# One two-bank PSUM tile, or two one-bank tiles, for the value product of a memory-attention and SwiGLU kernel

## The chip, the cores and the metric

The kernel runs on one core of one Trainium2 chip. The metric is the device time of one execution in microseconds (us). Before the change, three runs gave 909.52, 909.95 and 912.1 us, a median of 909.95 us.

The engines are PE (TensorE, matrix products, with the loads of its stationary operand listed as PEld), DVE (VectorE), ACT (ScalarE), POOL (GpSimd) and SP (which only issues DMAs here). Each engine runs its own instructions strictly in order. SBUF is the on-chip working memory, PSUM the memory that PE writes its results to: 8 banks of 2 KB in each of 128 partitions. POOL doesn't read PSUM in this kernel, so every result of PE is fetched by ACT or DVE.

## What is computed

```
# q, k, v: (8, 8, 576, 64), phi: (8, 8, 576, 32); w_gate, w_val: (512, 1536); w_out: (1536, 512)
a   = softmax(phi over its memory axis)
k_m = einsum('bhsm,bhsd->bhmd', a, k)
v_m = einsum('bhsm,bhsd->bhmd', a, v)
x   = softmax(q @ k_m^T / sqrt(64)) @ v_m          # as 4608 tokens x 512
xn  = x / rms(x) * rms_g
out = (silu(xn @ w_gate) * (xn @ w_val)) @ w_out
```

## The kernel before

**Tiling.** Eight batches are taken as four pairs of two batches (`pr`), with a pass of two pairs at a time. A first stage, up to about 148 us of the profile, reduces k, v and phi to k_m and v_m and prepares the attention weights of the first two pairs. The main loop follows: 48 steps `i`, each for one pair and one block `j` of 128 of the 1536 columns. The attention weights and the scores of the second pass are computed beside the first 24 or so steps, and the 64-bit weights of the inputs are turned into float32 there as well.

**High and low parts.** Every float32 operand of a product is split into a rounded high part and the rest, its low part, and a product is three matmuls: high by high, high by low, low by high. The high part is an ACT copy (a cast), the low part a subtraction on DVE (where the source is in PSUM) or on POOL (where it is in SBUF).

**A step of the main loop.** The names that follow are those of the profile.

- `vw_steps(i)`, the value product: v_m of two batches (`vm`) times a block of w_gate and w_val (`wh`, `wl`), into the PSUM tile `vp` (L840). It has 12 matmuls of 256 columns in two halves `cc`: `mm(0)` does the six of one, `mm(1)` the six of the other. `vp` is one tile of 4 KB in each partition, that is two banks, one for each `cc`, and there is one such tile (`bufs=1`). `evac` then takes it to SBUF: for rows 0 to 63, an ACT cast of both banks to `xh` (L853) and a DVE subtraction to `xl` (L854), then the same for rows 64 to 127.
- `gv_steps(i)`: `xh` and `xl` times the attention weights (`ath`, `atl`) give `pg` (gate) and `pv` (value) in PSUM (L876), for two batches and two groups of tokens. ACT takes the Silu of `pg` to `sg` (L884), DVE multiplies `pv` by it into `hf` (L885), ACT and POOL split that into `hh` and `hl` (L898, L899).
- `out_steps(i)`, after every second step: `hh`, `hl` times w_out (`oh`, `ol`) into `po` (L918), which ACT copies to the running sum `acc` the first time (L923) and DVE adds to it later (L925).

**Beside the steps.** `convert` turns a block of weights from its 64-bit form into float32 by five DVE operations on `ex` and `mi` (L345, L365, L347, L369, L358), two ACT ones (L350, L376) and a DVE product `w` (L385); ACT and POOL then split it into `wh`, `wl` or `oh`, `ol` (L402, L403). `attend_steps` does the scores of the second pass: transposes `qtp`, scores `S` on PE, their maximum `mx` (L992) and difference (L993) on DVE, and an exponential on ACT.

**What sets the order.** Each step has a place in time from a table of numbers (`PRM`), by which the steps are sorted and issued, once. A scheduler with a timeline of its own then sets the order in which each engine gets its instructions, from the dependencies and the buffers. So where the tiles change, it may put other instructions in other places too. Reads of the same PSUM tile by ACT and DVE are put one after the other: the second cast of a tile waits for the first subtraction.

**PSUM.** `g`, `v` and `o` (that holds `po`, `qtp`, `S`) have two banks each and `vw` has two: all eight are in use.

Of the kernel before, what the change touches and what calls it, by code (L numbers as in the profile page):

```python
# [8 lines left out]
F32 = mybir.dt.float32  # L9
# [4 lines left out]
ALU = mybir.AluOpType  # L14
# [76 lines left out]
def kernel(  # L91
# [25 lines left out]
    nc = tc.nc  # L117
    P = 128
# [309 lines left out]
    with ExitStack() as c1:  # L428
        sb = c1.enter_context(tc.tile_pool(name="sb1", bufs=2, reuse_waits="tile"))
        ps = c1.enter_context(tc.tile_pool(name="ps1", bufs=2, space=PSUM, reuse_waits="tile"))  # L430
# [341 lines left out]
        for b in range(B):  # L772
# [11 lines left out]
            else:  # L784
                p0 = PRM["PH"][b - 2] + PRM["PD"][b - 2]
                ev += place(p0, PRM["PREP"], preps[b][:5])
                e = max(K_AT[b - 2] + 6 * PRM["KP"], p0 + PRM["PREP"][-1]) + PRM["EXP"][b - 2]
# [25 lines left out]
    ps = ctx.enter_context(tc.tile_pool(name="ps2", bufs=2, space=PSUM, reuse_waits="tile"))  # L813

    NS = (NP // G) * NU * G * 2
    vw, hsplit, accs = {}, {}, {}

    def where(i):

        ps_, r = divmod(i, NU * G * 2)  # L820
        u, r = divmod(r, G * 2)
        pi, f = divmod(r, 2)
        return ps_, u, ps_ * G + pi, 2 * u + f

    def vw_steps(i):

        ps_, u, pr, j = where(i)

        def mm(cc):
            def f():  # L830
                if cc == 0:
                    vw[i] = [ps.tile([P, 2, 2, 256], F32, tag="vw", name=f"vp{i}", bufs=1)]
                vp = vw[i][0]
                vh, vl = vm[pr][:, 0], vm[pr][:, 1]
                wh, wl = (x.rearrange("p hp g f -> p hp (g f)") for x in wsplit[ps_ * NJ + j])
                for e in range(2):
                    def lhs(vt):
                        return vt[:, cc, e].rearrange("p o x -> p (o x)")
                    for n, (l, r) in enumerate(((vh, wh), (vh, wl), (vl, wh))):
                        nc.tensor.matmul(  # L840
                            vp[:, cc, e, :], lhs(l), r[:, 2 * cc + e, :],
                            start=(n == 0), stop=(n == 2),
                        )
            return f

        def evac():
            vp = vw[i][0]
            xh = sb.tile([P, 2, 2, 256], F32R, tag="xh", name=f"xh{i}", bufs=2)
            xl = sb.tile([P, 2, 2, 256], F32R, tag="xl", name=f"xl{i}", bufs=2)
            for h in range(2):  # L850
                rows = slice(64 * h, 64 * h + 64)
                src = vp[rows, :, ::-1, :] if h else vp[rows]
                nc.scalar.copy(xh[rows], src)  # L853
                nc.vector.tensor_tensor(out=xl[rows], in0=src, in1=xh[rows].bitcast(F32), op=ALU.subtract)  # L854
            vw[i] = xh, xl
        return [mm(0), mm(1), evac]

# [248 lines left out]
```

## Time and profile before

| | |
|---|---|
| median of 3 runs | 909.95 us (909.52 to 912.1) |
| the profiled execution | 910.09 us |
| its span, first to last instruction | 908.3 us |
| mean granted TensorE clock | 0.969 |
| `xh` casts on ACT (L853) | 96 of 64x1024, 96.6 us |
| `xl` subtractions on DVE (L854) | 96 of 64x1024, 117.2 us |
| `vp` matmuls on PE (L840) | 576 of 128x256 |

How to read it. A row of a group ends in the busy time of all its instructions, the mean of one in ns, and the time that the engine sat idle just before them. A wait names the engine that waited, and what it waited for, with the total, the number of times and the longest. In the view of windows, each row has a stretch of the span, its length, and the busy time of each engine in it with the number of instructions, then the granted clock of PE. Matmuls overlap, so a busy PE is one that has a matmul under way. The times of runs are some 1.8 us longer than the span, which starts with the first instruction.

### The profile page before, as it was taken

Reading aid. Unit: us, or ns where it says so; the run is one execution under the profiler, and the core shown is the slowest. Engines: PE = TensorE matmul, PEld = TensorE weight load, DVE = VectorE, ACT = ScalarE, POOL = GpSimd, SP = SyncE. Lnnn points to the kernel's source line nnn. Section 1 sums busy time; section 2 is a strip of 40 time slices with the busy share of each in tenths; the row PEclk is TensorE's granted clock in tenths of the full one; section 3 lists DMA queues with packets and bytes.
Section 4 is the critical chain, followed back from the end, with each engine's and each line's share of the span. In section 5 each row is a group of like instructions: output and inputs, shape, how many; then the busy total and the mean of one; then the engine's idle time right before and its main releaser. Section 6 shows DMA issues by size and latency. Waiting matters only on the chain.

```text
span 908.3 us, 15828 instructions
## 1 busy us (share of the span) xinstructions
PE 838.9 (92%) x6207; PEld 744.3 (82%) x6207; DVE 592.2 (65%) x1026; ACT 421.1 (46%) x717; POOL 286.6 (32%) x242
## 2 busy tenths in 40 slices
PE   4989485899989999899999999999999999999997
PEld 3777474889887899788888997798889999999996
DVE  5577968997898877988754655632445455454543
ACT  2656433777766464665543343254424333243330
POOL 3463745333333324234242241412112121121120
PEclk9889887999999999999999999999999999999999
DMA  8976543553464341634214134411204012040046
GB/s 284 324 254 236 201 157 96 182 185 86 153 166 132 106 119 61 165 110 153 89 58 140 35 94 128 97 55 47 93 1 140 1 48 93 1 140 1 1 111 144
DMA packets 81506, 106.41 MB, mean 117 GB/s; under 512 B 34324, under 2 KB 52248, under 8 KB 81432
## 3 DMA queue, kind: packets, MB, share of 16 engines
q1 hardware_dynamic: 81432, 105.41, 37.6%
q8 instruction: 49, 0.80, 0.4%
q14 instruction: 25, 0.20, 0.1%
HBM read 73.93 MB, written 31.46 MB: 116 GB/s over the span
## 4 chain that ended last, share of the span: by engine, by line
PE 74%; DVE 14%; issue 4%; DMA 4%; ACT 3%; POOL 1%; SPq 0%; DVEq 0%; ACTq 0%; POOLq 0%
PE po L918 29%; PE pv L876 14%; PE pg L876 14%; PE vp L840 7%; PE kvp L573 3%; PE xp L235 1%; DVE mi L365 1%; DVE xl L854 1%; DVE ex L345 1%; DVE w L385 1%; ACT xh L853 1%; PE qtp L685 1%; DVE mi L369 1%; DVE acc L925 1%; DMA phi<-in_phi_dram 1%
## 5 line engine op out<-in xcount | busy, mean ns | idle before, releaser
L899 POOL TENSOR_TENSOR hl<-hf,hh 128x512 fp32r<-128x512 f32 (+1 forms) x96 | 139.6, 1454 | 410.9 <-ACT hh L898 399.6
L925 DVE TENSOR_TENSOR acc<-po,acc 128x512 f32<-128x512 f32 x180 | 123.1, 687 | 130.2 <-PE po L918 129.5
L918 PE MATMUL po<-oh,hh 128*128 128x512 f32 x432 | 173.6, 403 | 3.6 <-DVE acc L925 2.6
L918 PE MATMUL po<-oh,hl 128*128 128x512 f32 x432 | 171.1, 396 | 0.0
L918 PE MATMUL po<-ol,hh 128*128 128x512 f32 x432 | 170.9, 396 | 0.0
L884 ACT ACTIVATE sg<-pg 128x256 f32<-128x256 f32 x192 | 77.7, 409 | 163.2 <-PE pg L876 144.2
L854 DVE TENSOR_TENSOR xl<-vp,xh 64x1024 fp32r<-64x1024 f32 x96 | 117.2, 1220 | 45.9 <-ACT xh L853 44.4
L885 DVE TENSOR_TENSOR hf<-pv,sg 128x256 f32<-128x256 f32 x192 | 85.3, 453 | 73.0 <-PE pv L876 51.1
L853 ACT CAST xh<-vp 64x1024 fp32r<-64x1024 f32 x96 | 96.6, 1007 | 51.7 <-PE vp L840 21.6
L898 ACT CAST hh<-hf 128x512 fp32r<-128x512 f32 (+1 forms) x96 | 64.6, 673 | 82.3 <-DVE hf L885 57.0
L918 PEld LDWEIGHTS po<-oh,hl 128*128 128x128 f32 x432 | 81.5, 189 | 19.5
L918 PEld LDWEIGHTS po<-oh,hh 128*128 128x128 f32 x432 | 81.5, 189 | 19.3 <-DVE acc L925 4.5
L876 PE MATMUL pg<-ath,xh 128*128 128x320 f32 (+1 forms) x384 | 86.6, 299 | 7.9 <-ACT xh L853 6.3
L918 PEld LDWEIGHTS po<-ol,hh 128*128 128x128 f32 x432 | 81.7, 189 | 11.5 <-DMA ol<-od 0.2
L840 PE MATMUL vp<-wh,vm 128*128 128x256 f32 x384 | 85.5, 288 | 4.8 <-DVE at L212 2.3
L876 PE MATMUL pv<-ath,xh 128*128 128x320 f32 (+1 forms) x384 | 84.7, 300 | 4.7 <-DVE hf L885 4.6
L876 PE MATMUL pg<-ath,xl 128*128 128x320 f32 (+1 forms) x384 | 85.7, 296 | 0.0
L876 PE MATMUL pv<-atl,xh 128*128 128x320 f32 (+1 forms) x384 | 84.7, 296 | 0.0
L876 PE MATMUL pg<-atl,xh 128*128 128x320 f32 (+1 forms) x384 | 84.4, 297 | 0.0
L876 PE MATMUL pv<-ath,xl 128*128 128x320 f32 (+1 forms) x384 | 83.3, 296 | 0.0
L876 PEld LDWEIGHTS pg<-ath,xh 128*128 128x128 f32 x384 | 63.8, 190 | 13.3 <-ACT xh L853 6.6
L840 PEld LDWEIGHTS vp<-wh,vm 128*128 128x128 f32 x384 | 66.0, 191 | 8.4 <-DVE xl L854 3.0
(129 smaller groups left out, 1377.5 us busy)
## 6 DMA issues: line engine op xcount, KB each, us to landing
kv<-in_k_dram SPq DMA_DIRECT2D x32, 288.0 KB, 4.8
kv<-in_v_dram SPq DMA_DIRECT2D x32, 288.0 KB, 5.4
out_dram<-acc SPq DMA_DIRECT2D x72, 128.0 KB, 2.4
raw<-in_moe_w_gate_dram SPq DMA_DIRECT2D x12, 512.0 KB, 4.8
raw<-in_moe_w_val_dram SPq DMA_DIRECT2D x12, 512.0 KB, 3.7
wd<-wh SPq DMA_DIRECT2D x12, 512.0 KB, 3.0
wd<-wl SPq DMA_DIRECT2D x12, 512.0 KB, 4.1
raw<-in_moe_w_out_dram SPq DMA_DIRECT2D x12, 512.0 KB, 3.6
```

What stands on the lines that cost most here:

```text
L235: nc.tensor.matmul(xp[64 * j:64 * j + 64, P * cc:P * cc + P], st["at"][:, t, cc, 64 * j:64 * j + 64], gb[:, j, cc], start=True, stop=True,)
L573: nc.tensor.matmul(kvp[64 * par:64 * par + 64, cc, 0:128], e_bd[j][:, hp, c, :], st["kv", b, hp][:, :, 64 * c:64 * c + 64], start=(c == 0) ...
L840: nc.tensor.matmul(vp[:, cc, e, :], lhs(l), r[:, 2 * cc + e, :], start=(n == 0), stop=(n == 2),)
L853: nc.scalar.copy(xh[rows], src)
L854: nc.vector.tensor_tensor(out=xl[rows], in0=src, in1=xh[rows].bitcast(F32), op=ALU.subtract)
L876: nc.tensor.matmul(pt[:, :N], l[:, cc, b, half * P:half * P + P], r[:, b, cc, t0:t0 + n, :].rearrange("p t x -> p (t x)"), start=(m == 0), ...
L884: nc.scalar.activation(sg[:, :N], pg[:, :N], AF.Silu)
L885: nc.vector.tensor_tensor(out=hf[:, :, b, :], in0=pv[:, :N].rearrange("p (t x) -> p t x", x=64), in1=sg[:, :N].rearrange("p (t x) -> p t x ...
L898: nc.scalar.copy(hh, hv)
L899: nc.gpsimd.tensor_tensor(out=hl, in0=hv, in1=hh.bitcast(F32), op=ALU.subtract)
L918: nc.tensor.matmul(po, l[:, tt, :], r, start=(m == 0), stop=(m == 5))
L925: nc.vector.tensor_tensor(out=accs[key], in0=po, in1=accs[key], op=ALU.add)
```

## The change

`vp` becomes two tiles of one bank, `vp_0` and `vp_1`, one for each `cc`, from a pool of two such buffers (`bufs=2`, the same two banks). Each is evacuated by itself: two ACT casts of 64x512, one for each half of the partitions, then two DVE subtractions of 64x512. The 48 steps so have 192 casts and 192 subtractions in place of 96 and 96, over as many elements. A bank is given back once its own two subtractions are done.

```diff
         def mm(cc):
             def f():
-                if cc == 0:
-                    vw[i] = [ps.tile([P, 2, 2, 256], F32, tag="vw", name=f"vp{i}", bufs=1)]
-                vp = vw[i][0]
+                vp = ps.tile([P, 2, 256], F32, tag="vw", name=f"vp{i}_{cc}", bufs=2)
+                vw.setdefault(i, []).append(vp)
                 vh, vl = vm[pr][:, 0], vm[pr][:, 1]
...
                         nc.tensor.matmul(
-                            vp[:, cc, e, :], lhs(l), r[:, 2 * cc + e, :],
+                            vp[:, e, :], lhs(l), r[:, 2 * cc + e, :],
                             start=(n == 0), stop=(n == 2),
                         )
             return f
 
         def evac():
-            vp = vw[i][0]
             xh = sb.tile([P, 2, 2, 256], F32R, tag="xh", name=f"xh{i}", bufs=2)
             xl = sb.tile([P, 2, 2, 256], F32R, tag="xl", name=f"xl{i}", bufs=2)
-            for h in range(2):
-                rows = slice(64 * h, 64 * h + 64)
-                src = vp[rows, :, ::-1, :] if h else vp[rows]
-                nc.scalar.copy(xh[rows], src)
-                nc.vector.tensor_tensor(out=xl[rows], in0=src, in1=xh[rows].bitcast(F32), op=ALU.subtract)
+            for cc, vp in enumerate(vw[i]):
+                halves = ((slice(0, 64), vp[:64]), (slice(64, P), vp[64:, ::-1, :]))
+                for rows, src in halves:
+                    nc.scalar.copy(xh[rows, cc], src)
+                for rows, src in halves:
+                    nc.vector.tensor_tensor(
+                        out=xl[rows, cc], in0=src, in1=xh[rows, cc].bitcast(F32), op=ALU.subtract
+                    )
             vw[i] = xh, xl
```

In the changed kernel the `vp` matmuls are at L839, the casts at L851 and the subtractions at L853, and all later lines of the main loop stand one further (L876 is L877, L884 is L885, and so on). The number at the end of a name in the rows below tells the buffers apart.

The scheduler's order changes from the first step of the main loop on. The first place is ACT at the first evacuation, where the loop begins. Before:

```order
L223 CAST ath_1783<-at_1503 128x2x64 x2
L350 ACTIVATE ex_0_1828<-ex_0_1828 128x512
L853 CAST xh_1822<-vp_1809 64x1024
L376 ACTIVATE mi_0_1833<-mi_0_1833 128x512
L853 CAST xh_1822<-vp_1809 64x1024
L402 CAST oh_2027<-w_0_1839 128x512
L350 ACTIVATE ex_1_1969<-ex_1_1969 128x512
```

And now:

```order
L223 CAST ath_1783<-at_1503 128x2x64 x2
L851 CAST xh_1823<-vp_0_1809 64x512 x2
L350 ACTIVATE ex_0_1833<-ex_0_1833 128x512
L851 CAST xh_1823<-vp_1_1816 64x512 x2
L376 ACTIVATE mi_0_1838<-mi_0_1838 128x512
L402 CAST oh_2042<-w_0_1844 128x512
L851 CAST xh_1899<-vp_0_1846 64x512 x2
L885 ACT_TABLE_LOAD
L885 ACTIVATE sg_00_1868<-pg_00_1854 128x256
```

The first bank's casts stand ahead of the conversion's `ex_0`, the second bank's ahead of `mi_0`; the next step's first bank (`vp_0_1846`) is cast ahead of the first Silu.

The second place is PE right behind the first value product, in the same stretch. Before:

```order
L840 MATMUL vp_1809<-wh_1363,vm_456 128x256
L876 MATMUL pg_00_1849<-ath_1393,xh_1822 128x256 x2
L876 MATMUL pg_00_1849<-atl_1394,xh_1822 128x256 x2
L876 MATMUL pv_00_1850<-ath_1393,xh_1822 128x256 x2
L876 MATMUL pv_00_1850<-atl_1394,xh_1822 128x256 x2
```

And now:

```order
L839 MATMUL vp_1_1816<-wh_1363,vm_456 128x256
L877 MATMUL pg_00_1854<-ath_1393,xh_1823 128x256
L877 MATMUL pv_00_1855<-ath_1393,xh_1823 128x256
L877 MATMUL pg_01_1871<-ath_1393,xh_1823 128x256
L877 MATMUL pv_01_1872<-ath_1393,xh_1823 128x256
L839 MATMUL vp_0_1846<-wh_1720,vm_456 128x256
L877 MATMUL pg_00_1854<-ath_1393,xh_1823 128x256
L877 MATMUL pg_00_1854<-atl_1394,xh_1823 128x256 x2
L877 MATMUL pg_00_1854<-ath_1393,xl_1824 128x256
```

Four matmuls that need only the first bank's high part come first, then one of the next step's value product, which needs the first bank given back, and only then those that need the second bank.

The third place is DVE shortly after the first subtractions, up to the first product `hf`. Before:

```order
L347 TENSOR_SCALAR ex_1_1969<-ex_1_1969 128x512
L369 SCALAR_TENSOR_TENSOR mi_1_1980<-raw_1741,mi_1_1980 128x512
L358 SCALAR_TENSOR_TENSOR ex_1_1969<-raw_1741,ex_1_1969 128x512
L385 TENSOR_TENSOR w_1_1986<-mi_1_1980,ex_1_1969 128x512
L345 TENSOR_SCALAR ex_2_2057<-raw_1836 128x512
L365 TENSOR_SCALAR mi_2_2062<-raw_1836 128x512
L347 TENSOR_SCALAR ex_2_2057<-ex_2_2057 128x512
L369 SCALAR_TENSOR_TENSOR mi_2_2062<-raw_1836,mi_2_2062 128x512
L885 TENSOR_TENSOR hf_0_1848<-pv_00_1850,sg_00_1863 128x4x64
```

And now:

```order
L347 TENSOR_SCALAR ex_1_1980<-ex_1_1980 128x512
L369 SCALAR_TENSOR_TENSOR mi_1_1995<-raw_1741,mi_1_1995 128x512
L853 TENSOR_TENSOR xl_1900<-vp_0_1846,xh_1899 64x512 x2
L886 TENSOR_TENSOR hf_0_1853<-pv_00_1855,sg_00_1868 128x4x64
L886 TENSOR_TENSOR hf_0_1853<-pv_01_1872,sg_01_1885 128x4x64
L358 SCALAR_TENSOR_TENSOR ex_1_1980<-raw_1741,ex_1_1980 128x512
```

The rest of the conversion of `ex_1`, and four operations of that of `ex_2`, stand behind the first `hf` now, and the next step's first two subtractions ahead of it.

## The prediction

> **What bounds the kernel now.** I read the page first, then the view of windows with one stretch for each stage of the main loop, then the waits of PE.
>
> ```profile
> span 908.3 us, 15828 instructions
> PE 838.9 (92%) x6207; PEld 744.3 (82%) x6207; DVE 592.2 (65%) x1026; ACT 421.1 (46%) x717; POOL 286.6 (32%) x242
> ```
>
> ```profile
> 148.00:222.00 74.00, 63.25 (x445) 58.06 (x445) 66.01 (x97) 51.07 (x89) 29.86 (x22) 0.91 0.54 161
> 222.00:300.00 78.00, 71.59 (x504) 62.31 (x499) 69.89 (x111) 52.04 (x87) 30.36 (x22) 1.00 0.48 145
> 300.00:908.00 608.00, 594.00 (x3792) 530.40 (x3791) 351.01 (x590) 248.32 (x420) 155.32 (x120) 1.00 0.28 82
> ```
>
> The busy columns are PE, PEld, DVE, ACT, POOL, then the granted clock. From 300 us on PE is busy 594.0 of 608 us while DVE has work for 58% of the time and ACT for 41%: PE sets the end, and what the change adds on DVE and ACT there lies beside PE. Before 300 us it is mixed: PE lacks 10.8 us in the first window and 6.4 in the second, and DVE is at 89% and 90%. PE still has all its later work ahead of it, so a microsecond of idle PE that goes there is a microsecond off the end, and one that comes is one on it. These are the waits of PE from 148 to 300 us (total, times, longest), and the one row on `vp` after 300:
>
> ```profile
> PE pg L876 <- ACT xh L853: 6.3, 1, 6.3
> PE pv L876 <- DVE hf L885: 4.1, 3, 2.2
> PE po L918 <- DVE acc L925: 1.9, 2, 1.7
> PE pg L876 <- ACT sg L884: 1.5, 1, 1.5
> PE vp L840 <- DVE xl L854: 1.2, 1, 1.2
> PE qtp L964 <- ACT acc L923: 0.7, 1, 0.7
> PE vp L840 <- DVE xl L854: 1.1, 2, 0.9
> ```
>
> The largest is a single wait of 6.3 us, at the first evacuation. There is no such wait at any of the 47 later ones: the steps overlap by then.
>
> **The change, part by part.** All sums are made against the profiled execution's own 910.09 us (span 908.3), which is 0.14 us above the median of the three runs.
>
> *The pieces.* What the two forms cost is read from these groups:
>
> ```profile
> L853 ACT CAST xh<-vp 64x1024 fp32r<-64x1024 f32 x96 | 96.6, 1007 | 51.7 <-PE vp L840 21.6 <-DVE xl L854 20.6 <-PE pv L876 8.6
> L854 DVE TENSOR_TENSOR xl<-vp,xh 64x1024 fp32r<-64x1024 f32 x96 | 117.2, 1220 | 45.9 <-ACT xh L853 44.4
> L923 ACT COPY acc<-po 128x512 f32<-128x512 f32 x36 | 21.0, 585 | 13.4 <-PE po L918 13.1
> L925 DVE TENSOR_TENSOR acc<-po,acc 128x512 f32<-128x512 f32 x180 | 123.1, 687 | 130.2 <-PE po L918 129.5
> ```
>
> A 64x512 cast or subtraction out of PSUM isn't in this trace. The nearest rows read 512 elements of each partition from PSUM as well: 585 ns on ACT, 687 on DVE. The lower end is half of the old ones, 504 and 610 ns. I take the nearest rows. Two new casts then cost 163 ns more than an old one, two subtractions 154 ns more; over 96 pairs that is 15.6 us of ACT and 14.8 us of DVE, or nothing at the lower end. Where they fall decides.
>
> *The first evacuation.* The timeline there (start, duration, engine; the bracket is the idle time before):
>
> ```profile
> 150.18 0.41 PE L840 MATMUL vp<-wh,vm 128*128 128x256 f32 x1
> 152.08 1.75 DVE L369 SCALAR_TENSOR_TENSOR mi<-raw,mi 128x512 f32<-128x512 uint32 x1
> 152.19 0.63 ACT L350 ACTIVATE ex<-ex 128x512 int32<-128x512 int32 x1 [3.22 <-DVE ex L347]
> 152.73 0.99 ACT L853 CAST xh<-vp 64x1024 fp32r<-64x1024 f32 x1
> 153.76 0.94 DVE L358 SCALAR_TENSOR_TENSOR ex<-raw,ex 128x512 int32<-128x512 int32 x1
> 154.62 1.21 DVE L854 TENSOR_TENSOR xl<-vp,xh 64x1024 fp32r<-64x1024 f32 x1
> 155.86 1.01 ACT L853 CAST xh<-vp 64x1024 fp32r<-64x1024 f32 x1 [1.30 <-DVE xl L854]
> 156.92 0.79 PE L876 MATMUL pg<-ath,xh 128*128 128x256 f32 x2 [6.32 <-ACT xh L853]
> ```
>
> The product is complete at 150.6, but the first cast stands behind L350, which waits 3.2 us for DVE, and the second cast waits for the first subtraction, which itself stands behind L369 and L358 on DVE. In the new order the first bank's casts are ahead of L350, on an ACT that has nothing else to do: done well before 152. L350 runs at 152.19 as before, and the second bank's casts follow it, needing nothing of DVE: from 152.8 to 154.0 with 2 x 0.585. So the high part is complete 2.9 us earlier. PE doesn't get all of it: ahead of the second bank's matmuls stands one of the next value product, which needs the first bank back. DVE is free for its two subtractions when L369 ends, at 153.83; they end at 153.83 + 2 x 0.687 = 155.2. PE goes on there, not at 156.92: **1.7 us**. Four matmuls were done in the gap, at the half clock of that stretch 0.21 us each (below): **0.85 us**. The second bank's subtractions end near 157.5 (L358 0.94, then 1.37), ahead of PE, which has 22 matmuls until it needs them. So 2.5 us at the restart; the bounds are 0 and the whole wait, 6.3.
>
> *Up to 222 us.* Not all 2.5 pass the first Silu:
>
> ```profile
> 155.75 0.67 DVE L385 TENSOR_TENSOR w<-mi,ex 128x512 f32<-128x512 f32 x1
> 161.37 0.62 ACT L402 CAST oh<-w 128x512 fp32r<-128x512 f32 x1 [0.90 <-DVE w L385]
> 162.01 1.28 ACT L884 ACT_TABLE_LOAD   x1
> 163.31 0.66 ACT L884 ACTIVATE sg<-pg 128x256 f32<-128x256 f32 x2
> 164.24 0.54 PE L876 MATMUL pg<-ath,xh 128*128 128x320 f32 x2
> ```
>
> The fifth `pg` needs the first one read by that Silu. ACT has two more casts ahead of the table load now, of a bank that PE fills until about 160.2: casts to 161.4, table to 162.65, Silu to 163.0. PE starts at 163.1 in place of 164.24, a lead of 1.1 us. After that DVE has less in front of `hf`: six conversion operations now stand behind the first `hf`, at 526 to 950 ns each,
>
> ```profile
> L347 DVE TENSOR_SCALAR ex<-ex 128x512 int32<-128x512 int32 x36 | 18.9, 526 | 0.0
> L385 DVE TENSOR_TENSOR w<-mi,ex 128x512 f32<-128x512 f32 x34 | 32.3, 950 | 3.1 <-POOL ol L403 1.1 <-ACT mi L376 0.6 <-POOL wl L403 0.3
> ```
>
> about 4.4 us at the middle, against two subtractions more, 1.4 us, and 0.3 for the split. So `hf` and `sg` come some 2.5 us earlier beside PE's lead of 1.1, and what PE waits for from 170 to 191 us can go: `sg` 1.5, two of the three `hf` waits (4.1 less the longest, 2.2), and `qtp` 0.7, together 4.1 us. The weights that are converted later are first needed by the fifth step, whose value product starts here:
>
> ```profile
> 207.31 0.28 PE L840 MATMUL vp<-wh,vm 128*128 128x256 f32 x1
> ```
>
> That is over 40 us later, so six operations that move by a few places don't delay it. I take 2.9 of the 4.1, for a lead of **4.0 us** at 222; the bounds up to there are 0 and 10.4, all waits of PE in it with the 6.3.
>
> *From 222 to 300 us.*
>
> ```profile
> 222.17 0.49 DVE L992 TENSOR_REDUCE mx<-S 128x10 f32<-128x320 f32 x1 [5.38 <-PE S L982]
> 222.00:300.00 78.00, 12.20 (x10) 1.00 0.48 145
> ```
>
> DVE has been idle for 5.4 us when `S` lands, so it can follow a lead of PE. From there it works nearly without a break, and PE waits for it: 2.2 us for `hf`, 1.9 for `acc`, 1.2 for `xl`. The second row is the window of L854 alone: ten subtractions, that become twenty and cost 10 x 0.154 = **1.5 us** more, all on the chain while DVE is late. Bounds: 0, and the 1.5 with the 1.8 of the twelve subtractions ahead of 222, that may cost the lead as much.
>
> *The waits on `vp`.* 1.2 and 1.1 us for a bank that now comes back sooner; bounds 0 and 2.3, and I take **0.5**, as the first lies in DVE's late stretch.
>
> *The rest.* After 300 us the added ACT and DVE time (74 of 96 evacuations) has PE's work as its cover; gone would be that cover only if DVE's 58% came near 100. DMAs are the same ones.
>
> The sum: 910.09 - 4.0 + 1.5 - 0.5 = **907.1 us**, 0.3% below the median, which is also what a measurement of this kernel can tell from no change (2.7 us).
>
> **A rule on the clock.** PE ran at half clock after its restart (the first row is a window, 0.50 its clock):
>
> ```profile
> 158.00:160.00 2.00, 2.00 (x11) 2.00 (x11) 1.87 (x4) 0.78 (x2) 0.87 (x1) 0.50 0.95 181
> ...
> 162.20 0.63 PE L876 MATMUL pv<-ath,xl 128*128 128x256 f32 x2
> 162.63 0.47 PE L876 MATMUL pg<-ath,xl 128*128 128x256 f32 x2
> 162.93 0.40 PE L876 MATMUL pv<-ath,xl 128*128 128x256 f32 x2
> 163.17 0.28 PE L840 MATMUL vp<-wh,vm 128*128 128x256 f32 x1
> ```
>
> Two matmuls take 0.43 us from start to start, the next two 0.30, the next 0.24: the clock came back at 162.6, 5.7 us after PE's restart, in which some 27 matmuls took 0.21 us each in place of 0.12, 2.5 us too long in all. In the sum I let the delay stay 5.7, so it moves with the restart. [...]
>
> **The rivals.**
>
> 1. *The clock comes back sooner after the restart, and all of the later waits go.* Half of the 2.5 us above are 1.25, and the 1.2 us left of the 4.1 are gone too: 907.1 - 2.45 = 904.6. For it: the wait at the restart is shorter and broken by five matmuls. Against: the first Silu holds PE whatever its clock. Chance 0.13. [...]
> 2. *The lead is given back.* DVE sets the pace through 300 us; conversions that are only put off come back in front of `mx` at 222 and of `acc` behind it, and slow down there as the 1.75 us of L369 above shows against the mean of such an operation. The lead of 4.0 shrinks to 1 or 2, the 1.5 stay: 909 to 911. That the change doesn't do what it says, because the casts stand behind other work in ACT's queue, ends at the same place. For it: DVE's 89 and 90%. Chance 0.27.
> 3. *Slower: DVE is the bound from 148 to 300 us and gains nothing.* The split adds 22 x 0.154 = 3.4 us there (12 subtractions before 222, ten after), and no wait of PE goes. This decides if DVE doesn't idle for 5.4 us ahead of `mx` at 222, since then PE's lead has been lost to it: 910.09 + 3.4 = 913.5. For it: every order of the loop changes, and one that makes PE wait for a bank or a weight costs the same. Against: 6.3 us in one place with a known cause. Chance 0.18.
>
> **How the numbers follow.** The forecast, from 905 to 909.2, has 0.42. Faster by over 0.3% means below 907.2: rival 1 and two thirds of the forecast, 0.42 with rounding. Within 0.3%: the rest of the forecast and nearly all of rival 2, 0.40. Slower, above 912.7: rival 3, 0.18. The range goes from 902.5, rival 1 with the 2.3 us of the `vp` waits gone as well, to the 913.5 of rival 3; what lies outside has some 0.2.
>
> **What would show it.** Right: 64x512 casts near 585 ns and subtractions near 687; one wait of some 4 us for `xh` or `xl` near 151 us in place of 6.3; PE's waits for `sg` and `hf` between 170 and 191 gone; a later total of waits after 300 us as small as now. Wrong: DVE with no idle time ahead of the second `mx`; new waits of PE for `acc` or `hf` between 222 and 300 us of more than 1.5 us; waits for `xl` after 300.

## The result: 1% slower, and the profile after

| | before | changed |
|---|---|---|
| median | 909.74 us (905.5 to 912.1, 6 runs) | 919.07 us (916.58 to 920.93, 6 runs) |
| ratio | | 1.0103, 95% interval 1.0073 to 1.0132 |
| profiled execution | 910.09 us, span 908.3 | 916.58 us, span 914.8 |
| mean granted clock | 0.969 | 0.977 |

The forecast was 907.1 us with a range up to 913.5, so the time lies outside it, on the slower side. The page of the changed kernel opens with the span and the busy time of the engines:

```profile
span 914.8 us, 16046 instructions
...
PE 837.9 (92%) x6207; PEld 741.2 (81%) x6207; DVE 615.9 (67%) x1122; ACT 438.9 (48%) x813; POOL 285.9 (31%) x242
```

PE does the same work in the same busy time (838.9 before); DVE has 23.7 us more, ACT 17.8. The groups of the two new operations, with the matmuls that wait for them:

```profile
L853 DVE TENSOR_TENSOR xl<-vp,xh 64x512 fp32r<-64x512 f32 x192 | 132.0, 687 | 27.6 <-ACT xh L851 25.5
...
L851 ACT CAST xh<-vp 64x512 fp32r<-64x512 f32 x192 | 111.6, 581 | 18.6 <-PE pv L877 10.0
...
L839 PE MATMUL vp<-wh,vm 128*128 128x256 f32 x384 | 88.5, 288 | 11.0 <-DVE xl L853 8.7
```

So the subtractions account for 14.8 of DVE's 23.7 us (132.0 against 117.2) and leave 8.9 that the diff doesn't explain. The windows by stage (PE, PEld, DVE, ACT, POOL, then the clock):

```profile
148.00:222.00 74.00, 64.15 (x462) 57.98 (x461) 69.73 (x111) 53.83 (x101) 26.92 (x20) 0.97 0.52 156
222.00:300.00 78.00, 68.61 (x473) 59.02 (x471) 66.77 (x116) 51.00 (x90) 29.18 (x21) 1.00 0.48 145
300.00:460.00 160.00, 150.32 (x1014) 133.41 (x1015) 135.09 (x230) 90.75 (x163) 48.24 (x35) 0.99 0.35 107
```

And the waits of PE from 148 to 300 us, then the largest after 300 us (total, times, longest):

```profile
PE vp L839 <- DVE xl L853: 5.0, 4, 3.2
PE po L919 <- DVE ex L994: 3.5, 3, 1.4
PE po L919 <- DVE acc L926: 2.7, 2, 1.5
PE pv L877 <- DVE hf L886: 2.4, 4, 1.0
PE pg L877 <- ACT sg L885: 2.2, 2, 1.4
PE po L919 <- ACT acc L924: 1.3, 1, 1.3
```

```profile
PE vp L839 <- DVE xl L853: 3.7, 4, 2.1
PE pv L877 <- DVE hf L886: 2.5, 4, 0.9
PE qtp L965 <- DVE acc L926: 2.3, 2, 2.0
```

The 6.3 us wait for `xh` is gone, 3.2 us for `xl` stand in its place, and the rest is many waits of about 1 us for what DVE makes: `ex`, `acc`, `hf`, `xl`. They go on after 300 us.

One caution about two single executions: the main loop (first matmul of `vp`) began at 144.67 us in the changed kernel and at 148.31 before, although the first stage is the same in both. (In the runs below it began anywhere from 142.7 to 149.4 us.) From there to the end of the span the changed kernel took 770.1 us and the kernel before 760.0. So the loop lost 10.1 us in this pair, more than the spans show, and the windows above compare stretches that lie 3.6 us apart in the loop. Counted from each loop's start in matmul work (each matmul taken at the median distance of starts of its kind in the kernel before), PE of the changed kernel is level with the kernel before at 74 and at 110 us, 4.4 us behind at 152, 11.1 at 312 and 10.2 at the end. The 152 and 312 us are 300 and 460 us in the profile of before.

### The profile page after: what moved, and what is told of

It reads as the page before. It is cut to its first block, busy times and chain, and to the rows that moved or that the text cites. A ratio compares the mean times of both kernels' runs of the same rounds, so it can differ in the third digit from the quotient of the medians.

```text
span 914.8 us, 16046 instructions
## 1 busy us (share of the span) xinstructions
PE 837.9 (92%) x6207; PEld 741.2 (81%) x6207; DVE 615.9 (67%) x1122; ACT 438.9 (48%) x813; POOL 285.9 (31%) x242
## 4 chain that ended last, share of the span: by engine, by line
PE 57%; DVE 9%; issue 7%; ACT 2%; POOL 1%; DVEq 0%; POOLq 0%; ACTq 0%
PE po L919 26%; PE pv L877 12%; PE pg L877 12%; PE vp L839 5%; DVE xl L853 2%; DVE acc L926 1%; DVE mi L369 1%; DVE mi L365 1%; DVE w L385 1%; DVE ex L345 1%; PE xp L235 1%; DVE hf L886 1%; DVE ex L358 0%; ACT L1001 0%; DVE ex L347 0%
## 5 line engine op out<-in xcount | busy, mean ns | idle before, releaser
L900 POOL TENSOR_TENSOR hl<-hf,hh 128x512 fp32r<-128x512 f32 (+1 forms) x96 | 140.4, 1463 | 428.5 <-ACT hh L899 407.3
L885 ACT ACTIVATE sg<-pg 128x256 f32<-128x256 f32 x192 | 77.8, 411 | 184.3 <-PE pg L877 163.3
L853 DVE TENSOR_TENSOR xl<-vp,xh 64x512 fp32r<-64x512 f32 x192 | 132.0, 687 | 27.6 <-ACT xh L851 25.5
L851 ACT CAST xh<-vp 64x512 fp32r<-64x512 f32 x192 | 111.6, 581 | 18.6 <-PE pv L877 10.0
L839 PE MATMUL vp<-wh,vm 128*128 128x256 f32 x384 | 88.5, 288 | 11.0 <-DVE xl L853 8.7
L899 ACT CAST hh<-hf 128x512 fp32r<-128x512 f32 (+1 forms) x96 | 64.5, 673 | 67.9 <-PE po L919 40.3
L877 PE MATMUL pv<-ath,xh 128*128 128x320 f32 (+1 forms) x384 | 85.9, 302 | 4.9 <-DVE hf L886 4.8
L877 PE MATMUL pg<-ath,xh 128*128 128x320 f32 (+1 forms) x384 | 86.9, 300 | 2.9 <-ACT sg L885 2.9
L877 PE MATMUL pg<-ath,xl 128*128 128x320 f32 (+1 forms) x384 | 84.8, 295 | 0.0
L877 PE MATMUL pv<-ath,xl 128*128 128x320 f32 (+1 forms) x384 | 84.1, 297 | 0.0
L877 PE MATMUL pv<-atl,xh 128*128 128x320 f32 (+1 forms) x384 | 83.5, 297 | 0.0
L877 PE MATMUL pg<-atl,xh 128*128 128x320 f32 (+1 forms) x384 | 83.5, 296 | 0.0
L839 PEld LDWEIGHTS vp<-wh,vm 128*128 128x128 f32 x384 | 66.9, 191 | 15.2 <-issue 6.6
L877 PEld LDWEIGHTS pv<-ath,xh 128*128 128x128 f32 x384 | 63.6, 190 | 12.2 <-DVE hf L886 5.9
```

Of the source, the lines that this page charges most:

```text
L839: nc.tensor.matmul(vp[:, e, :], lhs(l), r[:, 2 * cc + e, :], start=(n == 0), stop=(n == 2),)
L851: nc.scalar.copy(xh[rows, cc], src)
L853: nc.vector.tensor_tensor(out=xl[rows, cc], in0=src, in1=xh[rows, cc].bitcast(F32), op=ALU.subtract)
L877: nc.tensor.matmul(pt[:, :N], l[:, cc, b, half * P:half * P + P], r[:, b, cc, t0:t0 + n, :].rearrange("p t x -> p (t x)"), start=(m == 0), ...
L885: nc.scalar.activation(sg[:, :N], pg[:, :N], AF.Silu)
L899: nc.scalar.copy(hh, hv)
```

## The experiments

In all of them "order" is the sequence in which each engine gets its instructions. It was forced where that is said: after the program is written out, each instruction is tied to the one that shall stand ahead of it on its engine, with no wait added.

```diff
         tile_mem_attention_swiglu_kernel(tc, *args)
+        _pin(tc, nc)
```

All ratios are to runs of the kernel before on the same chip and in the same series.

| run | tiles | pieces | order | median us | ratio (95%) |
|---|---|---|---|---|---|
| x3_split_old_order | one | 64x512 | old | 910.22 | 1.0003 (0.9987 to 1.0018) |
| x1_two_tiles_old_order | two | 64x512 | old | 912.31 | 1.0029 (1.0013 to 1.0044) |
| x2_one_tile_new_order | one | 64x1024 | new | 968.02 | 1.0644 (1.0620 to 1.0668) |
| x4_casts_first_old_order | one | 64x1024 | old | 951.75 | 1.0465 (1.0442 to 1.0488) |
| x7_new_then_old | two | 64x512 | new to 222 us | 911.90 | 1.0038 (1.0022 to 1.0054) |
| x8_old_then_new | two | 64x512 | new from 222 us | 921.17 | 1.0140 (1.0114 to 1.0166) |
| x12_first_step_new | two | 64x512 | new to 170 us | 913.85 | 1.0054 (1.0034 to 1.0073) |
| x13_new_to_300 | two | 64x512 | new to 300 us | 912.38 | 1.0033 (1.0019 to 1.0047) |
| x14_old_to_300 | two | 64x512 | new from 300 us | 920.74 | 1.0123 (1.0100 to 1.0146) |
| x11_split_free | one | 64x512 | scheduler's own | 914.91 | 1.0081 (1.0049 to 1.0113) |
| n1_before_late_evac | one | 64x1024 | scheduler's own, came out as the old | 909.55 | 0.9996 (0.9981 to 1.0011) |
| n3_after_late_evac | two | 64x512 | scheduler's own, came out as the new | 919.34 | 1.0110 (1.0087 to 1.0134) |
| n4_after_early_evac | two | 64x512 | scheduler's own, came out as the new | 919.43 | 1.0105 (1.0081 to 1.0129) |
| x15_new_subs_up | two | 64x512 | new, subtractions up | 923.30 | 1.0158 (1.0130 to 1.0185) |
| x17_old_subs_up | two | 64x512 | old, subtractions up | 918.74 | 1.0095 (1.0067 to 1.0124) |
| x18_before_subs_up | one | 64x1024 | old, subtractions up | 918.15 | 1.0081 (1.0051 to 1.0110) |
| y1_before_no_pool | one | 64x1024 | old | 887.63 | 0.9759 (0.9740 to 0.9778) |
| y2_after_no_pool | two | 64x512 | new | 889.30 | 0.9793 (0.9767 to 0.9819) |

**The edit apart from the order.** First the pieces alone, in the place of the old ones:

```diff
-                nc.scalar.copy(xh[rows], src)
-                nc.vector.tensor_tensor(out=xl[rows], in0=src, in1=xh[rows].bitcast(F32), op=ALU.subtract)
+                for cc in range(2):
+                    nc.scalar.copy(xh[rows, cc], src[:, cc])
+                for cc in range(2):
+                    nc.vector.tensor_tensor(
+                        out=xl[rows, cc], in0=src[:, cc], in1=xh[rows, cc].bitcast(F32), op=ALU.subtract
+                    )
```

> One tile as before and the order as before, but each cast and subtraction of 64x1024 split into two of 64x512. It changes the number of pieces alone: theory of the pieces 6 to 9 us slower than before, theory of the order within 3 us. Against the run with two tiles in the old order it shows what the second tile brings: less waiting between ACT and DVE, 0 to 3 us faster with two tiles.

Measured: 1.0003. Then the whole change with the old order forced (the first bank's two casts stand where the first cast stood, and so on):

> The changed kernel's two tiles and split evacuation, with every engine's instructions held in the order of the kernel before (each old cast replaced by the two of one bank, each old subtraction by the two of one bank). Theory of the pieces (192 subtractions of 687 ns and 192 casts of 581 in place of 96 of 1220 and 1007 cost 0.15 us for each old one, on a DVE that sets the pace up to 450 us): 6 to 9 us slower than before, like the changed kernel. Theory of the order (the pieces are hidden, the scheduler's new order costs the time): within 3 us of before. If both carry a part: 3 to 6 us slower.

Measured: 1.0029. So 96 casts and 96 subtractions more, about 15 us on each of ACT and DVE, cost nothing that can be measured, and two tiles cost some 0.3%. The other 0.7 of the 1.0% come with the order that the scheduler made of them. The two counterparts keep one tile:

> The kernel before, one tile of two banks and 96 casts and subtractions, with every engine's instructions held in the order of the changed kernel (a cast or a subtraction of a half stands where the second one of a bank stood). Theory of the pieces: within 3 us of before, since no instruction is added. Theory of the order: 5 to 10 us slower than before; more than that if the one tile is given back later than the new order reckons with, so that PE waits longer for vp than the 11 us of the changed kernel.

> One tile, 64x1024 pieces and the order as before, but both casts of a tile come ahead of both subtractions, so that the second cast no longer waits for the first subtraction on DVE. Both theories: no pieces and no order change, so 0 to 3 us faster than before, mostly by the 6.3 us wait at the first evacuation, which should shrink to some 4.

```diff
+            halves = ((slice(0, 64), vp[:64]), (slice(64, P), vp[64:, :, ::-1, :]))
-            for h in range(2):
...
+            for rows, src in halves:
                 nc.scalar.copy(xh[rows], src)
+            for rows, src in halves:
                 nc.vector.tensor_tensor(out=xl[rows], in0=src, in1=xh[rows].bitcast(F32), op=ALU.subtract)
```

Both are far slower, the second against its expectation. The waits of `x4` on DVE, then the largest wait of PE in `x2`:

```profile
DVE xl L854 <- ACT xh L852: 134.3, 47, 5.7
```

```profile
PE vp L840 <- DVE xl L854: 28.0, 13, 4.3
```

In `x4` every first subtraction waits for both casts of the tile, though the second one's place on ACT is late; DVE idled 45.9 us ahead of all the subtractions before and waits 134.3 for casts here. In `x2` PE is sent to a bank that comes back only with the whole tile. These orders each belong to their own tiles; neither says anything about the 1% beyond that.

**Where in the order the loss lies.** Hybrids of the two orders, two tiles in all of them, cut by what stands ahead of a moment in the profiled run of `x1`:

> Two tiles; every instruction that stands in the first 222 us of the profiled run of the two-tile kernel in the old order is issued in the new order, all later ones in the old order. Two tiles in the old order took 912.3 us, in the new order 919.1. Theory E (the order loses its time in the first steps, where the conversions w on DVE come 5 to 10 us later): 917 to 919 us. Theory L (it loses it later, where DVE has the partial sums acc, the exponents ex and the subtractions together): 911 to 913. Theory S (both, in shares): 914 to 916.

> The counterpart: two tiles, old order up to 222 us, new order from there. Theory E: 911 to 913 us. Theory L: 918 to 920. Theory S: 914 to 916. If the two hybrids lose more together than the new order alone (6.8 us), the seam itself costs.

> Two tiles; only what stands in the first 170 us of the run in the old order (the first evacuation and the first Silu) is in the new order, all else in the old one. If the first evacuation's gain of some 1.6 us is kept by the order that follows it: 909 to 911 us. If it is given back at the next waits for sg and hf: 912 to 913. If the conversions put behind the first hf are what costs: 915 or more.

> Two tiles, the new order for what stands in the first 300 us of the run in the old order, the old order from there. New up to 222 us and old from there gave a ratio of 1.0038 to the kernel before, all new 1.0103, old up to 222 us and new from there 1.0140. If most of the loss is made between 222 and 300 us (waits of po for acc and ex, 6.7 us in the changed kernel): 1.008 to 1.011. If most of it is made after 300 us (waits of vp for xl and of pv for hf, 5 us more than before between 300 and 375 us): 1.003 to 1.006. Half and half: 1.006 to 1.008.

> Two tiles, old order for what stands in the first 300 us, the new order from there: the counterpart of the kernel with the new order up to 300 us (1.0033). Theory after 300 (the loss is made there, whatever stands ahead): a ratio of 1.009 to 1.013. Theory joint (the new order from 300 us costs only behind its own first part, which leaves DVE late): 1.003 to 1.006.

Measured: new up to 222 us 1.0038, up to 300 us 1.0033, neither to be told from no new order at all (1.0029); new from 222 us 1.0140, from 300 us 1.0123. What the new order loses beyond two tiles in the old one is made after 300 us, with either order ahead of it. The profiles say where: `x1`, `x13` and the changed kernel are 4.9, 3.0 and 4.4 us of matmul work behind the kernel before at 152 us into the loop, and 5.4, 3.5 and 11.1 at 312. (With the old order ahead, `x8` and `x14` lost more than the changed kernel's 1.0103, at the edge of what the intervals tell apart, so the seam may cost a little too. New only for the first step gave 1.0054, so the first evacuation's lead isn't kept by the order that follows it.) The waits of PE from 300 to 460 us in `x14`:

```profile
PE vp L839 <- DVE xl L853: 2.8, 2, 2.1
PE qtp L965 <- DVE acc L926: 2.3, 2, 2.0
PE po L919 <- DVE acc L926: 2.2, 4, 1.5
PE pv L877 <- DVE hf L886: 2.0, 3, 0.9
```

The longest are those of the changed kernel, number for number. They belong to that part of the order.

**Is it any new placing?** The scheduler was left free, with other pieces, and with one number of the table nudged:

```diff
-    VW=[-0.204, 0.03, 0.165],
+    VW=[-0.204, 0.03, 0.18],
```

> One tile of two banks, evacuated in the old order (cast, subtraction, cast, subtraction per pair) but in 64x512 pieces, as the run in the old order that took 910.2 us, here without a forced order: the scheduler places it. It never releases a bank early. If the order that comes of early release is what costs: 909 to 912 us. If any fresh placing by the scheduler (which reckons with the pieces' durations) costs several us against the old one: 914 to 920.

> The kernel before with one number of its table changed: the evacuation's place at 0.18 of a step in place of 0.165, so that the scheduler places everything after it anew; not an instruction is added or changed. Theory P (any fresh placing costs, since the order of before happens to be a good one): a ratio of 1.004 to 1.012, as the one tile in smaller pieces under the scheduler's own order (1.0081). Theory T (it is the order that comes of an early release of banks): 0.998 to 1.003.

> The changed kernel with the evacuation's place at 0.18 in place of 0.165: another placing of the same instructions. Theory P: anywhere between 1.002 and 1.016, since the loss is one of a particular placing. Theory T: 1.008 to 1.013, as the changed kernel (1.0103).

> The changed kernel with the evacuation's place at 0.16 in place of 0.165. Theory P: anywhere between 1.002 and 1.016, and not the same as with 0.18. Theory T: 1.008 to 1.013.

The nudges didn't do what they were meant to. In the traces of `n1`, `n3` and `n4` DVE, ACT and POOL have the very sequence of operations and tiles of the kernel that each was made from, and so has PE from the loop's first matmul on. They are repeats of the two kernels (0.9996, and 1.0110 and 1.0105 beside 1.0103) and say nothing of another placing. Fresh placings on record are only two, the changed kernel's and that of `x11`, and both lost. Early release isn't needed for a bad one: one tile in smaller pieces, placed by the scheduler, lost 0.8%, though the same pieces in the old order lost nothing. Whether any fresh placing loses, because the old order happens to be a good one (theory P), stays open.

**Late subtractions?** The longest wait after 300 us, as the changed kernel's timeline shows it (start, duration, engine):

```profile
351.00 2.38 ACT L851 CAST xh<-vp 64x512 fp32r<-64x512 f32 x4
...
351.49 1.77 DVE L385 TENSOR_TENSOR w<-mi,ex 128x512 f32<-128x512 f32 x1 [0.86 <-POOL wl L403]
353.29 0.43 DVE L345 TENSOR_SCALAR ex<-raw 128x512 int32<-128x512 int32 x1
353.64 0.42 DVE L365 TENSOR_SCALAR mi<-raw 128x512 int32<-128x512 int32 x1
353.97 0.42 DVE L347 TENSOR_SCALAR ex<-ex 128x512 int32<-128x512 int32 x1
354.31 1.78 DVE L369 SCALAR_TENSOR_TENSOR mi<-raw,mi 128x512 f32<-128x512 uint32 x1
356.01 1.38 DVE L853 TENSOR_TENSOR xl<-vp,xh 64x512 fp32r<-64x512 f32 x2
```

All casts are done at 353.38, but the subtractions that free the first bank stand behind conversions until 356.01, and PE goes on at 357.54 after 2.1 us. So three kernels had such subtractions moved up on DVE past the conversions ahead of them, where the casts were already done:

```diff
-        L385 w, L345 ex, L365 mi, L347 ex, L369 mi, L853 xl, L853 xl
+        L385 w, L853 xl, L853 xl, L345 ex, L365 mi, L347 ex, L369 mi
```

> The changed kernel in its own order, but from 222 us on each pair of subtractions on DVE is moved ahead of those conversion operations (w, ex, mi) directly in front of it that began after its casts had ended: 8 pairs are moved past 1 to 4 operations each, nothing else. Theory D (PE waits since the subtractions that free a bank stand behind conversions in the new order of DVE): the waits of vp for xl after 222 us (1.4 + 2.8 + 0.8 us) go, and the ratio falls from 1.0103 to 1.003 to 1.007. Theory M (PE's own order or the other waits cost, and these waits come back under other names): 1.008 to 1.012.

> Two tiles in the old order (1.0029), with 16 pairs of subtractions moved in the same way, past 1 to 5 conversion operations, from the first step on. Theory D: 0.999 to 1.002. Theory M: 1.002 to 1.004. If it is under 0.998, it beats the kernel before.

> The kernel before in its own order, with 15 of its 96 subtractions moved past 1 to 4 conversion operations in the same way. It has 2.1 us of waits of vp for xl after 222 us. Theory D: 0.996 to 0.999. Theory M: 0.999 to 1.002.

All three got slower, by 0.55% (1.0103 to 1.0158), 0.66% and 0.8%, beyond the ranges of both theories. Moving the subtractions up doesn't win the time back. In `x15` the wait that it aimed at did go, but others came (PE, 222 to 460 us; first the changed kernel, then `x15`):

```profile
PE vp L839 <- DVE xl L853: 4.2, 4, 2.1
PE po L919 <- DVE acc L926: 3.5, 5, 1.5
```

```profile
PE po L919 <- DVE acc L926: 5.5, 7, 1.5
PE pg L877 <- ACT sg L885: 2.6, 2, 2.3
...
PE S L983 <- DVE acc L926: 2.0, 1, 2.0
...
PE vp L839 <- DVE xl L853: 0.7, 1, 0.7
```

3.5 us for `xl` went, but `po` waits 2.0 us more for `acc`, `S` 2.0, and `pg` 2.6 for `sg`, which had 0.6 in the changed kernel. `po` waits 1.1 us less for `ex`, so in all the waits nearly cancel. Most of what is left of the loss in this pair is the clock. The same stretch in the changed kernel, then in `x15`, there with one wait in it and the 3.4 us behind that wait:

```profile
222.00:460.00 238.00, 218.93 (x1487) 192.43 (x1486) 201.86 (x345) 141.75 (x253) 77.42 (x56) 0.99 0.39 120
```

```profile
222.00:460.00 238.00, 218.01 (x1448) 191.61 (x1447) 200.02 (x337) 137.76 (x247) 76.42 (x56) 0.97 0.38 119
...
259.37 0.59 PE L877 MATMUL pg<-ath,xh 128*128 128x320 f32 x2 [2.26 <-ACT sg L885]
...
259.80:263.20 3.40, 3.40 (x16) 3.40 (x16) 3.37 (x8) 1.42 (x5) 0.00 (x0) 0.50 0.56 175
```

PE is busy as long, but with 39 matmuls fewer: behind the 2.3 us wait for `sg` it ran at half clock for 3.4 us. Over its loop `x15` has 25.6 us at half clock where the changed kernel has 12.0, and only 0.4 us more of idle PE (39.4 and 39.0). So more went there than the 2.3 us of the wait itself, and these runs don't show what late subtractions cost by themselves.

**What makes DVE so full.** In the timeline above, L385 and L369 took 1.77 and 1.78 us, while others of their kind take 0.7. POOL at that moment:

```profile
354.09 1.45 POOL L403 TENSOR_TENSOR wl<-w,wh 128x512 fp32r<-128x512 f32 x1 [1.39 <-ACT wh L402]
```

L369 began 0.22 us after it and ended 0.55 us behind its end (356.09 and 355.54). Of the conversion operations that began between 300 and 460 us, 18 in the changed kernel took over 0.15 us longer than the fastest of their line; each overlapped a POOL operation, and ended 0.55 us (L358, L369, L385) or 0.28 to 0.29 (L345, L365) after POOL's end. Before there were 12, each beside POOL's work too. The busy time of the six lines on DVE in that window, each from the view of windows for that line:

| us, 300 to 460 | L345 | L347 | L365 | L369 | L358 | L385 | sum (operations) |
|---|---|---|---|---|---|---|---|
| before | 7.82 | 5.88 | 6.51 | 12.13 | 10.09 | 12.99 | 55.4 (80) |
| changed | 7.34 | 5.42 | 9.66 | 11.17 | 11.74 | 15.94 | 61.3 (80) |
| x13, new to 300 | 8.97 | 7.26 | 5.43 | 11.74 | 10.12 | 12.36 | 55.9 (81) |
| x14, new from 300 | 7.37 | 5.79 | 10.71 | 12.72 | 11.76 | 15.92 | 64.3 (82) |

The two kernels with the new order after 300 us pay 6 to 9 us more than before (`x14` for two operations more), the one with the old order there 0.5. `x1`, with the old order throughout, has 57.3 for 82 operations, so `x14` pays 7.0 more for as many. Over the whole span the six lines take 157.5 us before and 166.1 in the changed kernel: 8.6 of the 8.9 us that the diff didn't explain. The last pair of runs takes POOL's subtractions (L403, and L899 or L900) out of both kernels, 132 operations; the matmuls take the high part in place of the low one:

```diff
             nc.scalar.copy(dh, src)
-            nc.gpsimd.tensor_tensor(out=dl, in0=src, in1=dh.bitcast(F32), op=ALU.subtract)
...
-                nc.gpsimd.tensor_tensor(out=hl, in0=hv, in1=hh.bitcast(F32), op=ALU.subtract)
-                hsplit[i, gi] = hh, hl
+                hsplit[i, gi] = hh, hh
```

> The kernel before in its own order, without the 132 POOL subtractions that make the low parts of the converted weights and of hf (L403, L899): the matmuls that took a low part take the high part in its place, so the counts on PE, DVE, ACT and the DMA queues stay. It is the yardstick for the next run. In the run of before, conversion operations on DVE took 40 us more than at their fastest, 31.6 of that beside these two POOL lines; that should fall to about 9. Time: 900 to 909 us in either theory.

> The changed kernel in its own order, without the same 132 POOL subtractions. Theory K (the new order puts more conversions beside POOL's work: 49.1 us of excess against 40.5, 7.2 of the difference between 300 and 460 us, and that is what its later part loses): 0 to 4 us above the run of before without them. Theory W (the order itself makes PE wait, whatever the conversions take): 7 to 11 us above it. Between, 4 to 7: both.

Measured: 887.63 and 889.30 us, 1.7 us apart in place of 9.3, as theory K had it; `y1` itself lies well below the 900 to 909 us that were expected. One conversion line in the changed kernel, then in `y1` and in `y2` (950 ns before):

```profile
L385 DVE TENSOR_TENSOR w<-mi,ex 128x512 f32<-128x512 f32 x34 | 35.1, 1033 | 2.8 <-POOL wl L403 1.0 <-ACT mi L376 0.8 <-POOL ol L403 0.4
```

```profile
L385 DVE TENSOR_TENSOR w<-mi,ex 128x512 f32<-128x512 f32 x34 | 24.8, 730 | 1.4 <-ACT mi L376 0.6
```

```profile
L385 DVE TENSOR_TENSOR w<-mi,ex 128x512 f32<-128x512 f32 x34 | 24.8, 731 | 1.9 <-ACT mi L376 1.4
```

And the window from 300 to 460 us in `y1` and in `y2`:

```profile
300.00:460.00 160.00, 157.21 (x1114) 141.66 (x1113) 115.01 (x214) 90.42 (x152) 6.37 (x8) 1.00 0.35 112
```

```profile
300.00:460.00 160.00, 157.19 (x1113) 141.54 (x1112) 118.97 (x232) 93.00 (x172) 6.34 (x8) 1.00 0.36 114
```

DVE's 129.66 us before and 135.09 in the changed kernel fall to 115.0 and 119.0, and PE is busy as long in both. Between 152 and 312 us into the loop, where PE lost 6.7 us of matmul work to the kernel before, it loses 1.1 in this pair. So most of the loss needs POOL's work beside DVE. What the pair doesn't part: without it DVE loses 31 to 38 us of stretched conversions over the span, and DVE's waits for POOL go as well (`hf` for `hl`, 14.2 us before and 18.6 in the changed kernel, and some such as the 0.86 us for `wl` above), so a full DVE and the 6 us that the new order adds to it are taken away together. Two kernels say that stretched conversions aren't the only way to lose: `x17` lost 0.66% to `x1` with conversions of 159.0 us over the span, against 156.9 there, and `x11` lost 0.8% with 158.0, 0.5 more than before. (`x18` has 161.7, so part of its loss may be of this kind.) That the new order's own 6 us make the larger part of its loss agrees with the four hybrids and the last pair, but wasn't tried by itself: it would need the new order with POOL's work shifted by a microsecond here and there.

No version that computes all of it was faster than the kernel before; the nearest is `x3` (`n1` being the kernel before once more).

## Why the prediction was wrong, step by step

- **The pieces: right.** 581 and 687 ns against 585 and 687 taken; 14.8 us on DVE and 15.0 on ACT (111.6 - 96.6) against 14.8 and 15.6. The lower end, half of the old durations, is ruled out.
- **The first evacuation: right in kind and size.** Counted from each loop's start, PE restarted 7.0 us in (151.67) in place of 8.6, a lead of 1.6 where 1.7 was taken, and the wait that stands there is 3.2 us for `xl`, as the step described. The first `pg` behind the Silu started at 159.00:

```profile
151.67 0.37 PE L839 MATMUL vp<-wh,vm 128*128 128x256 f32 x1 [3.18 <-DVE xl L853]
...
155.03 0.41 PE L877 MATMUL pv<-ath,xl 128*128 128x256 f32 x1
155.25 0.32 PE L839 MATMUL vp<-wl,vm 128*128 128x256 f32 x1
155.41 0.40 PE L839 MATMUL vp<-wh,vm 128*128 128x256 f32 x2
155.64 0.28 PE L839 MATMUL vp<-wl,vm 128*128 128x256 f32 x1
...
159.00 0.56 PE L877 MATMUL pg<-ath,xh 128*128 128x320 f32 x2 [1.37 <-ACT sg L885]
```

   That is 14.3 us into the loop, 15.9 before: a lead of 1.6, against 1.1. (The prediction's list of waits from 148 to 300 us lacks the 2.3 us of the loop's first matmul for `at`, which stand in both kernels; no term rests on it.)
- **The clock.** Starts lie 0.21 us apart up to 155.25 and 0.12 from 155.4: the clock came back 3.6 us after the restart, not 5.7, so the sum's constant was wrong, and that half of rival 1 came true. The 1.25 us that rival 1 gave it was somewhat too much by the prediction's own rows, as an estimate: 2.1 us less at half clock are some 10 matmuls that each lose 0.09 us, 0.9 us. Two restarts with two delays don't show what sets the delay.
- **The lead of 4.0 us at 222 us: wrong.** The waits went only in part (from 148 to 300 us 2.4 us in four for `hf`, 4.1 in three before, and 2.2 for `sg`, 1.5 before), and DVE's idle time ahead of the second `mx`, named as the sign, was gone:

```profile
219.53 1.39 DVE L853 TENSOR_TENSOR xl<-vp,xh 64x512 fp32r<-64x512 f32 x2 [1.37 <-ACT xh L851]
220.96 0.49 DVE L993 TENSOR_REDUCE mx<-S 128x10 f32<-128x320 f32 x1
```

   That `mx` is 76.3 us into the loop; before it was 73.9, so on DVE it lags by 2.4 us. PE, counted in matmul work, led by 2.4 us at 50 us into the loop and is level at 74: no lead in place of 4.0. The prediction counted what was taken from in front of `hf` as gain, and asked of what was put behind only when its weights are needed. It is right that no wait for weights came; but conversions then stood in front of `xl`, as the rows at 351 to 356 us show. That they did the same to `acc` and `ex` agrees with the waits, but isn't shown.
- **From 222 to 300 us, 1.5 us: the sign of a new wait came.** PE now waits for `ex` (3.5 us in three waits from 148 to 300 us, none before) and 0.8 us more for `acc`, and it is busy for 3.0 us less (68.61 against 71.59). Counted in matmul work it goes from level to 4.4 us behind between 74 and 152 us into the loop, nearly three times the 1.5 taken. The hybrids say that this isn't dearer than two tiles in the old order, which are 4.9 us behind by then in `x1` (1.0033 and 1.0029 in all).
- **The waits on `vp`, 0.5 us less: wrong.** 5.0 + 3.7 us, of which 3.2 at the first evacuation; the other 5.5 compare with 2.3 before.
- **"The rest": the step that failed.** "After 300 us the added ACT and DVE time (74 of 96 evacuations) has PE's work as its cover; gone would be that cover only if DVE's 58% came near 100." The 58% were a mean over one window of 608 us. The same view, cut where the conversions end, reads for the kernel before:

```profile
300.00:460.00 160.00, 154.11 (x1069) 137.00 (x1069) 129.66 (x220) 91.13 (x152) 53.90 (x40) 1.00 0.38 114
460.00:880.00 420.00, 416.22 (x2613) 373.84 (x2612) 210.35 (x354) 154.68 (x263) 98.57 (x79) 1.00 0.22 66
```

   DVE is at 81% in the first and at 50% in the second. The added pieces are indeed covered (`x3`), but the reordered work isn't: the new order from 300 us alone costs 0.94% (1.0123 against 1.0029), some 8.5 us, and in the changed kernel's own profile PE falls a further 6.7 us behind between 300 and 460 us of before, where the step had nothing. The term that was put at nothing is that of the new order, behind a DVE that had little room there.
- **The rivals.** Rival 3 had the side right, by another mechanism: its price was 0.154 us for each split subtraction while DVE is the bound, and `x3` has all of these at no cost. Rival 2 had the mechanism in a side remark, that conversions put off "slow down there", but only before 300 us, giving back 2 to 3 us of the lead.

## What to carry to other kernels

Where a scheduler places the work, an edit comes with a new order, and the two are to be costed apart: here the edit cost 0.3% and the order 0.7%. A run that is meant to try another placing has to be seen to have one: compare the sequences in the traces first. Read the cover for added work from the stage in which it falls, not from a mean that runs past it. And where DVE is full, count its operations at the duration that they have beside POOL (L385 took 1033 ns in the mean in the changed kernel, and 731 in `y2`), and look at which of them a new order puts there.

## What the runs showed of the hardware

- Nineteen conversions on DVE began while POOL worked, in the changed kernel from 300 to 460 us. They weren't slowed in proportion to the overlap: 18 of them ended 0.55 us or 0.28 to 0.29 us after POOL's end, however long the overlap, and their recorded durations grew accordingly (L385 to between 1.33 and 2.09 us, where its fastest took 0.67). The trace shows the times, not what held the operations. The other began within 0.01 us of POOL's operation (434.52 us) and took its usual 0.67; there POOL's took 2.11 us, against a mean of 1.60 for its kind.
- The size of it was not expected: without the 132 subtractions on POOL, an engine that is busy 32% of the span before, the kernel took 21.7 us less than 909.4 (`y1`). DVE's 14.2 us of waits for `hl` are in that.
- In the kernel before, PE was idle for 6.3 us and had its full clock back 5.7 us after the restart (156.92 and 162.6 us); in the changed kernel it was idle for 3.2 us and had it back after 3.6 (151.67 and 155.25 us). Behind an idle PE of 2.3 us the clock fell to a half only 0.4 us after the restart, for 3.4 us (`x15`, 259.8 us).
